# All tiles sum their attention scores in PSUM, and softmax reads them there

## The chip, the cores and the metric

The kernel runs on one core of a Trainium2 chip. Its time is the device time of one execution in microseconds (us), and several executions are compared by their median. A core has five engines with queues of their own: PE (matmuls, whose weight loads the profile shows as PEld), DVE (elementwise work and reductions), ACT (activation functions and copies), POOL, and SP, which here issues the DMAs. An engine takes its queue in order; semaphores hold an instruction until what it needs is done.

## What is computed

Attention over keys and values that are averaged in groups of 8, then two feed-forward layers over all 4608 tokens. All is float32.

```python
# attention: q, k, v of shape (8 batches, 8 heads, 576, 64)
k_p = k.reshape(B, H, Sp, 8, D).mean(axis=3)        # Sp = 72
v_p = v.reshape(B, H, Sp, 8, D).mean(axis=3)
scores = (1 / sqrt(D)) * q @ k_p.T                   # (8, 8, 576, 72)
scores = scores - max(scores, axis=-1)
attn = exp(scores); attn = attn / (sum(attn, -1) + 1e-9)
x = attn @ v_p                                       # as (4608, 512)
# first layer, 512 -> 768 -> 512
h = max(x @ w1, x @ w2, x @ w3); x = h @ w_out
# second layer, 512 -> 2048 -> 512
h = x @ w_in; x = (h - tanh(h)) @ w_out2
```

To keep float32 accuracy with the faster `float32r` matmuls, each operand is split in a high part H and a rest L, and a product is the sum of three matmuls: H·H, H·L and L·H.

## The kernel before

**Tiles.** The 576 tokens of a batch are cut into five tiles, four of 128 tokens and one of 64, in two units that meet where a block of 512 tokens of the next layer ends; 40 tiles in all, numbered from 0. A tile n is computed in two halves g = 0 and 1 of four heads each: `qk(n, g)` makes the scores of two pairs of heads (a pair p has 2 x 72 = 144 score columns), `sm_exp(n, g)` the maximum of each head (DVE, L304) and four exponentials with their sums (ACT, L307), `sm_div(n)` divides (DVE, L315 to L317) and copies the columns past 128 (ACT, L319), `tr(n)` transposes on PE (L335, L346) and splits the result (ACT L337 and L348, DVE L338 and L349). When a unit is through, `av` multiplies with the values (PE L356 to L359) and splits the output into the next layer's input (ACT L363, DVE L364).

**Two forms of `qk`.** The queries are the stationary operand: `qH` (128 rows, as many columns as the tile has tokens) is loaded into PE, and the keys `kbd` stream through it as two blocks of 144 columns, high and low part beside each other.

- The first 8 tiles (`NDIR = 8`) take the direct form: per pair three matmuls of 144 columns, qH·kH, qH·kL and qL·kH (L275 to L277), add up in one place of PSUM. Both pairs of a half share one PSUM tile of the pool `ps2` (tag `sc`, two buffers), and maximum and exponential read it there.
- The other 32 tiles take the form with two halves beside each other: one matmul of 288 columns gives qH·kH and qH·kL side by side (L283), one of 144 columns adds qL·kH to the first (L285). ACT copies the second half to SBUF (L287), DVE adds it to the first and writes the score to SBUF (L288), where maximum and exponential read it. Each pair takes a PSUM tile of its own, and it is free again after the addition.

**Order.** Attention, the preparation of weights and the first matmuls of the first layer run side by side. A list of steps (`qk`, `sm_exp`, `sm_div`, `tr`, `av`, loads) is worked off in pieces between the groups of the first layer (`moe_group`: 12 matmuls of 512 columns, L523 to L525, the result taken by ACT L527 or DVE L529), as `moe_part` paces it. Between them stand the steps of `Conv`, which turn 64-bit weights into float32: one ACT and four DVE instructions each (L94, L101 to L107) and for the first 18 weights a split (ACT L128, DVE L129). The builder's scheduler then puts the instructions of each engine into a final order, which need not be the order in which they were written. After the last tile come only matmuls with 512 columns: the rest of the first layer, its output (L657 to L659) and the second layer (L715 to L730).

Of the kernel before, what the change touches and what calls it, by code (L numbers as in the profile page):

```python
# [7 lines left out]
F32 = mybir.dt.float32  # L8
# [5 lines left out]
ALU = mybir.AluOpType  # L14
# [4 lines left out]
SP = S // POOL  # L19
# [4 lines left out]
NP = NH // 2  # L24
W2 = 2 * SP
# [9 lines left out]
NC2 = FF2 // 128  # L35
LAG = 3
LEAD = 0.3
NDIR = 8
RAWS = 3

TANH_T = 0.6
# [11 lines left out]
def moe_chain_kernel(ctx, tc, qt, kt, vm, vl, ident, cst, w123, wo1, win, wout, out):  # L53
    nc = tc.nc
    V, A, G, T, Q = nc.vector, nc.scalar, nc.gpsimd, nc.tensor, nc.sync
# [3 lines left out]
    def pool(name, bufs=1, side="left", **kw):  # L59
        cm = tc.tile_pool(name=name, bufs=bufs, side=side, **kw)  # L60
        stacks[name] = cm
        return cm.__enter__()
# [6 lines left out]
    ps2 = pool("ps2", bufs=2, space=PS)  # L69
# [70 lines left out]
    at = pool("at", side="right")  # L140
# [103 lines left out]
    qraw, qsp, sct, eT = {}, {}, {}, {}  # L244
# [19 lines left out]
    scp, nbs = {}, {}  # L264

    def qk(n, g):

        cnt = tiles[n][2]
        h, l = qsp[n]
        kb = kbd[tiles[n][0] % 2]  # L270
        if n < NDIR:
            ps = scp[n, g] = ps2.tile([128, 512], F32, tag="sc", name="ps_sc")
            for p in (2 * g, 2 * g + 1):
                o = ps[:cnt, p % 2 * W2:p % 2 * W2 + W2]
                T.matmul(o, h[:, p, :cnt], kb[:, p, 0], start=True, stop=False)  # L275
                T.matmul(o, h[:, p, :cnt], kb[:, p, 1], start=False, stop=False)
                T.matmul(o, l[:, p, :cnt], kb[:, p, 0], start=False, stop=True)  # L277
            return
        if g == 0:
            sct[n] = at.tile([128, NP, W2], F32, tag="sc", name="sc", bufs=2)  # L280
        for p in (2 * g, 2 * g + 1):
            ps = ps2.tile([128, 512], F32, tag="sc", name="ps_sc")
            T.matmul(ps[:cnt, :2 * W2], h[:, p, :cnt], kb[:, p].rearrange("p a k -> p (a k)"),  # L283
                     start=True, stop=False)
            T.matmul(ps[:cnt, :W2], l[:, p, :cnt], kb[:, p, 0], start=False, stop=True)  # L285
            tmp = at.tile([128, W2], F32, tag="sct", name="sct", bufs=2)
            A.copy(tmp[:cnt], ps[:cnt, W2:2 * W2])  # L287
            V.tensor_tensor(out=sct[n][:cnt, p], in0=ps[:cnt, :W2], in1=tmp[:cnt], op=ALU.add)  # L288

    lft = {}  # L290

    def sm_exp(n, g):
        cnt = tiles[n][2]
        if g == 0:
            if n < NDIR:
                sct[n] = at.tile([128, NP, W2], F32, tag="sc", name="sc", bufs=2)
            nbs[n] = (at.tile([128, NH], F32, tag="nb", name="nb", bufs=2),
                      at.tile([128, NH], F32, tag="su", name="su", bufs=2))
        s = sct[n][:cnt].rearrange("p c (h k) -> p (c h) k", k=SP)
        nb, su = (t[:cnt] for t in nbs[n])  # L300
        src = (scp.pop((n, g))[:cnt, :2 * W2].rearrange("p (h k) -> p h k", k=SP) if n < NDIR else
               s[:, 4 * g:4 * g + 4])
        c = slice(4 * g, 4 * g + 4)
        V.tensor_reduce(out=nb[:, c], in_=src, axis=AX.X, op=ALU.max, negate=True)  # L304
        for h in range(4):
            i = 4 * g + h
            A.activation(s[:, i], src[:, h], AF.Exp, bias=nb[:, i:i + 1], scale=1.0,  # L307
                         accum_out=su[:, i:i + 1])
# [108 lines left out]
    for n in range(ntl + 1):  # L417
        last = n == ntl
        if not last:
            b = tiles[n][0]  # L420
            k = n - first_tile[b]
# [10 lines left out]
        if not last:  # L432
            add(qk, n, 0)
            add(sm_exp, n, 0)
        if n:
            add(sm_div, n - 1)
        if not last:
            add(qk, n, 1)
            if aux:
                add(*aux.pop(0))  # L440
            add(sm_exp, n, 1)
# [268 lines left out]
    def h2(j, c):  # L710
        ps = psc.tile([128, 512], F32, tag="mm", name="ps_mm", bufs=3)
        wh, wl_ = (t.rearrange("p (a b) -> p a b", b=128) for t in wt[2 * c])
        for kc in range(NE):
            xh, xl2 = ct[j * NE + kc][0]
            T.matmul(ps, wh[:, kc], xh, start=(kc == 0), stop=False)  # L715
            T.matmul(ps, wh[:, kc], xl2, start=False, stop=False)  # L716
            T.matmul(ps, wl_[:, kc], xh, start=False, stop=(kc == NE - 1))  # L717
        return ps
# [22 lines left out]
    for i in range(len(seq) + LAG):  # L741
        if i < len(seq):
            j, c = seq[i]
            ps = h2(j, c)
# [67 lines left out]
```

## Time and profile before

| | |
|---|---|
| device time, median of 3 runs | 1552.76 us (1550.59 to 1554.56) |
| span of the profiled execution, first to last instruction | 1548.8 us |
| PE busy | 1508.3 us, 97% of the span |
| weight loads of PE (beside the matmuls) | 1250.4 us, 81% |
| DVE busy | 1154.0 us, 75% |
| ACT busy | 823.5 us, 53% |
| POOL busy | 195.5 us, 13% |

The span is one execution under the profiler; what lies around it (1552.76 - 1548.8 = 4.0 us against the median) is start and end of the program. Busy times of PE are the lengths of its matmuls as modelled, and these overlap; how much of PE's time a matmul takes is the distance from its start to the next one's. In the rows, "idle before" is the time in which the engine had nothing to run, and the name behind the arrow is what ended it.

### The profile page before, as it was taken

What the parts mean: (1) busy time and instruction counts of PE and PEld (TensorE: products, weight loads), DVE (VectorE), ACT (ScalarE), POOL (GpSimd) and SP (SyncE); (2) the same over time, 40 slices, a digit from 0 to 9 for tenths busy, and PEclk for the clock granted to TensorE, in tenths of its full rate; (3) what the DMA queues carried; (4) which work ended last, traced back from release to release, by engine and by line L of the source; (5) the groups of instructions that cost most, each with busy time, mean ns of one, the idle gap of its engine ahead of it and who ended that gap; (6) DMA issues with size and microseconds to landing.
All of it is one profiled execution on the core that took longest, in us unless ns stands there. A gap on an engine that the chain in (4) does not pass through costs nothing.

```text
span 1548.8 us, 20108 instructions
## 1 busy us (share of the span) xinstructions
PE 1508.3 (97%) x6896; PEld 1250.4 (81%) x6896; DVE 1154.0 (75%) x2050; ACT 823.5 (53%) x2059; POOL 195.5 (13%) x223
## 2 busy tenths in 40 slices
PE   4899999999999999999999999999999999999999
PEld 4678878888888788888888888888888888888887
DVE  7998378777777831533488888888888888888886
ACT  7664266555566510632455555555555555555554
POOL 4503020202100110920001000010101000010000
PEclk9889999999999999999999999999999999999999
DMA  7645144545332511955300000010100000010000
GB/s 260 182 136 173 58 138 145 173 147 180 123 120 96 182 50 51 328 188 174 123 1 28 28 28 28 1 55 0 55 1 28 28 28 28 0 55 0 28 1 28
DMA packets 68614, 134.55 MB, mean 87 GB/s; under 512 B 11552, under 2 KB 11680, under 8 KB 68512
## 3 DMA queue, kind: packets, MB, share of 16 engines
q1 hardware_dynamic: 68512, 133.27, 26.5%
q8 instruction: 54, 0.88, 0.2%
q14 instruction: 48, 0.39, 0.1%
HBM read 91.82 MB, written 41.42 MB: 86 GB/s over the span
## 4 chain that ended last, share of the span: by engine, by line
PE 89%; DVE 8%; ACT 1%; issue 1%; DMA 0%; ACTq 0%; DVEq 0%; SPq 0%
PE ps_mm L715 8%; PE ps_mm L717 8%; PE ps_acc L730 8%; PE ps_acc L728 8%; PE ps_acc L729 8%; PE ps_mm L716 8%; PE ps_mm L523 8%; PE ps_mm L524 8%; PE ps_mm L525 8%; PE ps_acc L659 2%; PE ps_acc L658 2%; PE ps_acc L657 2%; PE ps_mm L659 1%; PE ps_mm L658 1%; PE ps_mm L657 1%; PE ps_sc L283 1%
## 5 line engine op out<-in xcount | busy, mean ns | idle before, releaser
L523 PE MATMUL ps_mm<-xH,wH 128*128 128x512 f32 x648 | 260.0, 402 | 0.0
L524 PE MATMUL ps_mm<-xL,wH 128*128 128x512 f32 x648 | 254.2, 392 | 0.0
L525 PE MATMUL ps_mm<-xH,wL 128*128 128x512 f32 x648 | 253.8, 392 | 0.0
L703 ACT CAST gH<-w 128x512 fp32r<-128x512 f32 x144 | 89.4, 621 | 301.3 <-DVE w L702 301.3
L715 PE MATMUL ps_mm<-ioH,ctH 128*128 128x512 f32 x576 | 224.2, 389 | 0.8 <-ACT ioH L614 0.8
L717 PE MATMUL ps_mm<-ioH,ctL 128*128 128x512 f32 x576 | 224.1, 389 | 0.0
L716 PE MATMUL ps_mm<-ioL,ctH 128*128 128x512 f32 x576 | 224.1, 389 | 0.0
L728 PE MATMUL ps_acc<-ctH,gH 128*128 128x512 f32 x576 | 224.1, 389 | 0.0
L729 PE MATMUL ps_acc<-ctL,gH 128*128 128x512 f32 x576 | 224.1, 389 | 0.0
L730 PE MATMUL ps_acc<-ctH,gL 128*128 128x512 f32 x576 | 224.1, 389 | 0.0
L704 DVE TENSOR_TENSOR gL<-w,gH 128x512 fp32r<-128x512 f32 x144 | 103.9, 722 | 92.1 <-ACT gH L703 86.5
L529 DVE TENSOR_TENSOR h<-h,ps_mm 128x512 f32<-128x512 f32 x108 | 73.9, 685 | 104.2 <-PE ps_mm L525 102.9
L525 PEld LDWEIGHTS ps_mm<-xH,wL 128*128 128x128 f32 x648 | 121.9, 188 | 25.9
L615 POOL TENSOR_TENSOR ioL<-ioL,ioH 128x512 fp32r<-128x512 f32 x32 | 49.3, 1558 | 728.9 <-ACT ioH L614 728.9
L523 PEld LDWEIGHTS ps_mm<-xH,wH 128*128 128x128 f32 x648 | 122.6, 189 | 22.7
L524 PEld LDWEIGHTS ps_mm<-xL,wH 128*128 128x128 f32 x648 | 122.4, 189 | 22.5 <-DVE xL L364 0.3
L715 PEld LDWEIGHTS ps_mm<-ioH,ctH 128*128 128x128 f32 x576 | 108.2, 188 | 23.7 <-ACT ioH L614 1.2
L729 PEld LDWEIGHTS ps_acc<-ctL,gH 128*128 128x128 f32 x576 | 108.1, 188 | 22.6
L717 PEld LDWEIGHTS ps_mm<-ioH,ctL 128*128 128x128 f32 x576 | 108.1, 188 | 22.5
L730 PEld LDWEIGHTS ps_acc<-ctH,gL 128*128 128x128 f32 x576 | 108.1, 188 | 22.4
L716 PEld LDWEIGHTS ps_mm<-ioL,ctH 128*128 128x128 f32 x576 | 108.1, 188 | 22.4
L728 PEld LDWEIGHTS ps_acc<-ctH,gH 128*128 128x128 f32 x576 | 108.0, 188 | 22.3
(106 smaller groups left out, 2843.9 us busy)
## 6 DMA issues: line engine op xcount, KB each, us to landing
hs<-h SPq DMA_DIRECT2D x54, 256.0 KB, 2.0
ioL<-hs SPq DMA_DIRECT2D x54, 256.0 KB, 3.2
kraw<-kt SPq DMA_DIRECT2D x32, 288.0 KB, 3.3
raw<-w SPq DMA_DIRECT2D x18, 512.0 KB, 3.8
xs<-ob SPq DMA_DIRECT2D x36, 256.0 KB, 2.1
ioL<-xs SPq DMA_DIRECT2D x36, 256.0 KB, 3.4
out<-ob SPq DMA_DIRECT2D x36, 256.0 KB, 2.2
qraw<-qt SPq DMA_DIRECT2D x32, 256.0 KB, 3.0
```

The costliest lines, as they stand in the source:

```text
L523: T.matmul(ps[:, :BA], wH[i][:, kc], xh[:, kc], start=(kc == 0), stop=False)
L524: T.matmul(ps[:, :BA], wH[i][:, kc], xl[:, kc], start=False, stop=False)
L525: T.matmul(ps[:, :BA], wL[i][:, kc], xh[:, kc], start=False, stop=(kc == NE - 1))
L529: V.tensor_tensor(out=t, in0=t, in1=ps[:, :BA], op=ALU.max)
L703: A.copy(gH, w)
L704: V.tensor_tensor(out=gL, in0=w, in1=gH.bitcast(F32), op=ALU.subtract)
L715: T.matmul(ps, wh[:, kc], xh, start=(kc == 0), stop=False)
L716: T.matmul(ps, wh[:, kc], xl2, start=False, stop=False)
L717: T.matmul(ps, wl_[:, kc], xh, start=False, stop=(kc == NE - 1))
L728: T.matmul(acc, gH[:, r], oh, start=(c == 0), stop=False)
L729: T.matmul(acc, gH[:, r], ol, start=False, stop=False)
L730: T.matmul(acc, gL[:, r], oh, start=False, stop=(c == NC2 - 1))
```

## The change

`NDIR` and the second form are gone: all 40 tiles take the direct form. For the 32 tiles from the ninth on, each pair of heads has three matmuls of 144 columns where it had one of 288 and one of 144, the copy L287 and the addition L288 are gone, the two pairs of a half share one PSUM tile, and maximum (L304) and exponential (L307) read PSUM where they read SBUF. The exponential still writes `sc` in SBUF. Lines of the changed kernel after L290 have numbers that are lower by 15.

```diff
-NDIR = 8
     def qk(n, g):
...
-        if n < NDIR:
-            ps = scp[n, g] = ps2.tile([128, 512], F32, tag="sc", name="ps_sc")
-            for p in (2 * g, 2 * g + 1):
-                o = ps[:cnt, p % 2 * W2:p % 2 * W2 + W2]
-                T.matmul(o, h[:, p, :cnt], kb[:, p, 0], start=True, stop=False)
-                T.matmul(o, h[:, p, :cnt], kb[:, p, 1], start=False, stop=False)
-                T.matmul(o, l[:, p, :cnt], kb[:, p, 0], start=False, stop=True)
-            return
-        if g == 0:
-            sct[n] = at.tile([128, NP, W2], F32, tag="sc", name="sc", bufs=2)
+        ps = scp[n, g] = ps2.tile([128, 512], F32, tag="sc", name="ps_sc")
         for p in (2 * g, 2 * g + 1):
-            ps = ps2.tile([128, 512], F32, tag="sc", name="ps_sc")
-            T.matmul(ps[:cnt, :2 * W2], h[:, p, :cnt], kb[:, p].rearrange("p a k -> p (a k)"),
-                     start=True, stop=False)
-            T.matmul(ps[:cnt, :W2], l[:, p, :cnt], kb[:, p, 0], start=False, stop=True)
-            tmp = at.tile([128, W2], F32, tag="sct", name="sct", bufs=2)
-            A.copy(tmp[:cnt], ps[:cnt, W2:2 * W2])
-            V.tensor_tensor(out=sct[n][:cnt, p], in0=ps[:cnt, :W2], in1=tmp[:cnt], op=ALU.add)
+            o = ps[:cnt, p % 2 * W2:p % 2 * W2 + W2]
+            T.matmul(o, h[:, p, :cnt], kb[:, p, 0], start=True, stop=False)
+            T.matmul(o, h[:, p, :cnt], kb[:, p, 1], start=False, stop=False)
+            T.matmul(o, l[:, p, :cnt], kb[:, p, 0], start=False, stop=True)
...
     def sm_exp(n, g):
...
-            if n < NDIR:
-                sct[n] = at.tile([128, NP, W2], F32, tag="sc", name="sc", bufs=2)
+            sct[n] = at.tile([128, NP, W2], F32, tag="sc", name="sc", bufs=2)
...
-        src = (scp.pop((n, g))[:cnt, :2 * W2].rearrange("p (h k) -> p h k", k=SP) if n < NDIR else
-               s[:, 4 * g:4 * g + 4])
+        src = scp.pop((n, g))[:cnt, :2 * W2].rearrange("p (h k) -> p h k", k=SP)
```

The scheduler's order changes with it, from the tile numbered 8 (the ninth, of 64 tokens) on. Three places matter below.

On PE, one half of a tile of 128 tokens between matmuls of the first layer, before (a name is output<-inputs, and the size is the output's):

```order
L525 MATMUL ps_mm<-xH,wL_157 128x512
L283 MATMUL ps_sc<-kbd_167,qH 128x288
L285 MATMUL ps_sc<-kbd_167,qL 128x144
L283 MATMUL ps_sc<-kbd_167,qH 128x288
L285 MATMUL ps_sc<-kbd_167,qL 128x144
L523 MATMUL ps_mm<-xH,wH_139 128x512
```

and in the changed kernel (L273 to L275 are the three matmuls, L508 to L510 those of the first layer):

```order
L510 MATMUL ps_mm<-xH,wL_157 128x512
L273 MATMUL ps_sc<-kbd_167,qH 128x144
L274 MATMUL ps_sc<-kbd_167,qH 128x144
L275 MATMUL ps_sc<-kbd_167,qL 128x144
L273 MATMUL ps_sc<-kbd_167,qH 128x144
L274 MATMUL ps_sc<-kbd_167,qH 128x144
L275 MATMUL ps_sc<-kbd_167,qL 128x144
L508 MATMUL ps_mm<-xH,wH_139 128x512
```

Four matmuls have become six, and they still stand in one piece.

On DVE, from the division of tile 7 on (L317; L129, L103 and L105 prepare weights, L288 adds scores, L304 takes a maximum, L338 and L349 split the transposed tile 7), before:

```order
L317 TENSOR_TENSOR sc<-sc,su 128x576
L288 TENSOR_TENSOR sc<-ps_sc,sct 64x144
L129 TENSOR_TENSOR wL_154<-ma,wH_136 128x512
L103 TENSOR_SCALAR ma<-ma 128x512 x2
L288 TENSOR_TENSOR sc<-ps_sc,sct 64x144
L188 TENSOR_REDUCE ksum<-kraw 128x72
L304 TENSOR_REDUCE nb<-sc 64x4
L338 TENSOR_TENSOR eL<-ps_tr,eH 128x4x128
L349 TENSOR_TENSOR eX<-ps_tr,eX 32x2x128
L259 TENSOR_TENSOR qL<-qraw,qH 128x512
L188 TENSOR_REDUCE ksum<-kraw 128x72
L315 TENSOR_SCALAR su<-su 64x8
```

and in the changed kernel (L302 is the division, L289 the maximum, L323 and L334 the two splits, L128 and L104 prepare weights):

```order
L302 TENSOR_TENSOR sc<-sc,su 128x576
L187 TENSOR_REDUCE ksum<-kraw 128x72
L289 TENSOR_REDUCE nb<-ps_sc 64x4
L128 TENSOR_TENSOR wL_154<-ma,wH_136 128x512
L323 TENSOR_TENSOR eL<-ps_tr,eH 128x4x128
L334 TENSOR_TENSOR eX<-ps_tr,eX 32x2x128
L258 TENSOR_TENSOR qL<-qraw,qH 128x512
L187 TENSOR_REDUCE ksum<-kraw 128x72
L300 TENSOR_SCALAR su<-su 64x8
L104 SCALAR_TENSOR_TENSOR ma<-raw,ma 128x512
```

The additions are gone, the two L103 have moved behind the next division, and one L105 (now L104) has come forward. From here to the division of tile 8 both have the update of the keys (L201, now L200), the first maximum of tile 9 and a reciprocal; before it also two additions of scores, in the changed kernel also the second maximum of tile 9.

On DVE again, before the division of tile 16 (L317; ahead of it a group of the first layer, L529, and a preparation of weights, L101 to L107, with scores and a maximum of tile 17 in between), before:

```order
L316 RECIPROCAL su<-su 128x8
L529 TENSOR_TENSOR h<-h,ps_mm 128x512
L101 TENSOR_SCALAR ma<-ma 128x512
L288 TENSOR_TENSOR sc<-ps_sc,sct 64x144
L103 TENSOR_SCALAR ma<-ma 128x512
L288 TENSOR_TENSOR sc<-ps_sc,sct 64x144
L105 SCALAR_TENSOR_TENSOR ma<-raw,ma 128x512
L304 TENSOR_REDUCE nb<-sc 64x4
L107 SCALAR_TENSOR_TENSOR ma<-raw,ma 128x512
L317 TENSOR_TENSOR sc<-sc,su 128x576
```

and in the changed kernel (division L302; L514 is the group of the first layer, L323 and L334 split the transposed tile 15, the preparation begins with L100):

```order
L300 TENSOR_SCALAR su<-su 128x8
L301 RECIPROCAL su<-su 128x8
L302 TENSOR_TENSOR sc<-sc,su 128x576
L514 TENSOR_TENSOR h<-h,ps_mm 128x512
L323 TENSOR_TENSOR eL<-ps_tr,eH 128x4x128
L334 TENSOR_TENSOR eX<-ps_tr,eX 32x2x128
L187 TENSOR_REDUCE ksum<-kraw 128x72
L514 TENSOR_TENSOR h<-h,ps_mm 128x512
L100 TENSOR_SCALAR ma<-ma 128x512
```

The division stands right behind its sums and reciprocal now, ahead of the whole preparation of weights.

## Rows read from the trace of the kernel before

**Rows 1.** The page: the whole span.

```profile
span 1548.8 us, 20108 instructions
```

**Rows 2.** Busy time (instructions) of each engine by stretch, granted clock, DMA.

```profile
68.00:86.00 18.00, 11.67 (x53) 8.16 (x52) 17.16 (x39) 14.23 (x63) 8.54 (x15) 0.72 0.58 184
86.00:515.00 429.00, 422.75 (x2109) 352.57 (x2109) 325.89 (x728) 239.80 (x904) 49.99 (x84) 1.00 0.42 134
515.00:1548.80 1033.80, 1029.14 (x4539) 851.36 (x4538) 752.67 (x1163) 521.39 (x906) 106.32 (x70) 1.00 0.17 57
```

**Rows 3.** Waits of PE's weight loads, 68 to 515 us: total, times, longest.

```profile
PEld ps_sc L283 <- DVE sc L288: 5.3, 7, 1.8
PEld ps_av L356 <- DVE xL L364: 4.8, 7, 1.9
PEld ps_tr L335 <- DVE sc L317: 4.2, 3, 1.9
```

**Rows 4.** Timeline of PE: start, length, instruction; the direct form, six matmuls.

```profile
49.67 0.23 PE L275 MATMUL ps_sc<-kbd,qH 128*128 128x144 f32 x1
...
50.07 0.27 PE L276 MATMUL ps_sc<-kbd,qH 128*128 128x144 f32 x1
50.18 0.28 PE L277 MATMUL ps_sc<-kbd,qL 128*128 128x144 f32 x1
50.29 0.44 PE L523 MATMUL ps_mm<-xH,wH 128*128 128x512 f32 x1
```

**Rows 5.** Timeline of PE: the form with two halves, four matmuls, 128 tokens.

```profile
302.29 0.29 PE L283 MATMUL ps_sc<-kbd,qH 128*128 128x288 f32 x1
...
302.73 0.44 PE L523 MATMUL ps_mm<-xH,wH 128*128 128x512 f32 x1
```

**Rows 6.** Timeline of PE: the same form, 64 tokens.

```profile
314.90 0.29 PE L283 MATMUL ps_sc<-kbd,qH 128*64 128x288 f32 x1
315.04 0.23 PE L285 MATMUL ps_sc<-kbd,qL 128*64 128x144 f32 x1
...
315.30 0.44 PE L523 MATMUL ps_mm<-xH,wH 128*128 128x512 f32 x1
```

**Rows 7.** Groups by line and shape: count | busy us, mean ns | idle before.

```profile
L307 ACT ACTIVATE sc<-sc,nb 128x72 f32<-128x72 f32 x200 | 68.7, 345 | 36.1 <-DVE nb L304 36.1
L105 DVE SCALAR_TENSOR_TENSOR ma<-raw,ma 128x512 int32<-128x512 int32 x56 | 40.0, 716 | 0.2
L283 PE MATMUL ps_sc<-kbd,qH 128*128 128x288 f32 x100 | 29.2, 338 | 2.7 <-DVE sc L288 2.6
L288 DVE TENSOR_TENSOR sc<-ps_sc,sct 128x144 f32<-128x144 f32 x100 | 28.1, 301 | 18.0 <-ACT sct L287 17.5
L304 DVE TENSOR_REDUCE nb<-sc 128x4 f32<-128x288 f32 x50 | 22.4, 448 | 0.8
L307 ACT ACTIVATE sc<-ps_sc,nb 128x72 f32<-128x72 f32 x56 | 17.2, 324 | 1.9 <-DVE nb L304 1.9
L304 DVE TENSOR_REDUCE nb<-ps_sc 128x4 f32<-128x288 f32 x14 | 6.2, 444 | 0.4 <-PE ps_sc L277 0.3
```

**Rows 8.** Timeline of PE, waits at tiles 8 to 10 [idle before <-releaser].

```profile
76.54 0.61 PE L283 MATMUL ps_sc<-kbd,qH 128*128 128x288 f32 x1 [1.53 <-DVE sc L288]
79.33 0.70 PE L285 MATMUL ps_sc<-kbd,qL 128*128 128x144 f32 x2 [2.19 <-DVE qL L259]
...
82.91 0.69 PE L335 MATMUL ps_tr<-idt,sc 64*128 64x64 f32 x4 [1.14 <-DVE sc L317]
...
84.86 0.74 PE L356 MATMUL ps_av<-eH,VH 128*128 128x448 f32 x1
```

**Rows 9.** Timeline of DVE, from the division of tile 7 to that of tile 8.

```profile
72.71 1.08 DVE L317 TENSOR_TENSOR sc<-sc,su 128x576 f32<-128x576 f32 x1
...
74.53 1.74 DVE L103 TENSOR_SCALAR ma<-ma 128x512 int32<-128x512 int32 x2
76.19 0.29 DVE L288 TENSOR_TENSOR sc<-ps_sc,sct 64x144 f32<-64x144 f32 x1
...
82.11 0.74 DVE L317 TENSOR_TENSOR sc<-sc,su 64x576 f32<-64x576 f32 x1
```

**Rows 10.** Timeline of PE, two later waits.

```profile
212.84 0.36 PE L356 MATMUL ps_av<-eH,VH 128*128 128x192 f32 x1 [1.69 <-DVE xL L364]
...
229.09 0.66 PE L335 MATMUL ps_tr<-idt,sc 128*128 128x128 f32 x4 [1.55 <-DVE sc L317]
```

## The prediction

> **What bounds the kernel now.** I read the busy time by stretch first. From 515 us on PE runs 1029.1 of 1033.8 us [rows 2], on matmuls that the change does not touch; so the end moves by as much as PE reaches that point earlier or later. Ahead of it PE is idle for 6.3 us between 86 and 515 us and for another 6.3 between 68 and 86, where the granted clock averages 0.72, that is, a part of the stretch at the lower level of 1.2 GHz [rows 2]. The first eight tiles, up to 68 us, have the same form before and after, and their instructions stand in the same order. So the question is how many microseconds of PE's time the new form costs, and how many of these 12.6 idle ones it gives back. I read the waits next: PE's weight loads wait for the additions of scores (5.3 us), the split of the attention output (4.8) and the division (4.2), all on DVE [rows 3], which is busy 17.2 of the 18 us of the early stretch [rows 2].
>
> **PE pays.** The columns are the same: 288 + 144 before, 3 x 144 after. What is new is a matmul with a weight load per pair. The timeline shows both forms at the full clock. In the direct form the six matmuls of a half take from 49.67 to 50.29 us, 0.62 us until the next matmul starts, and they start 0.11 apart, which is more than 144 columns take (0.06, from the two starts below) and so is the load of 128 weight columns [rows 4]. In the form with two halves the four take from 302.29 to 302.73, 0.44 us [rows 5]. A half costs 0.18 us more. L283 ran 100 times on tiles of 128 tokens [rows 7], two to a half, so 50 halves: 50 x 0.18 = 9.0 us. In tiles of 64 tokens the four matmuls take 0.40 us (314.90 to 315.30), and one of 144 columns 0.06 with half as many weights to load (the second starts at 315.04 as the first of 288 columns took 0.14, and the four sum up as 0.14 + 0.06 twice) [rows 6]; six of them take 6 x 0.065 = 0.39, no more than before. The changed order keeps the six in one piece between matmuls of 512 columns, as it kept the four, so nothing hides the loads there. Four of the 50 halves (tiles 9 and 10) fall between 72 and 90 us, where PE waits for others: 0.7 us hidden. PE's share is **+8.3 us**, and this term is measured, not guessed; if nothing is hidden it is 9.0.
>
> At this place the Trainium skill speaks differently. Its page "TensorE: Matmul & The Clock Gate", section "Back-to-back issue gap", gives about 81 ns per matmul for a steady stream with 128 columns; by it six would take 0.49 us and the term would be 50 x 0.05 = 2.5 us. The 0.11 us between starts in rows 4 is what this kernel's `float32r` loads take, and I go by it.
>
> **What DVE and ACT save.** 128 additions at 0.30 us (the mean of L288 [rows 7]) leave DVE and as many copies leave ACT. The maximum costs the same from either memory (444 and 448 ns), the exponential is a little shorter from PSUM (324 against 345) [rows 7]. None of this counts by itself, since both engines are idle often; it counts where PE waits.
>
> **The stretch of tiles 8 to 10.** Here PE has done its matmuls of the first layer and waits in turn for additions, for the split of a query tile and for a division (1.53, 2.19 and 1.14 us), until the product with the values starts at 84.86 [rows 8]; from there on it is busy. The path runs over DVE from the division of tile 7 to that of tile 8, 72.71 to 82.11 us [rows 9]. By the two orders, four additions of this path go (4 x 0.30), the two L103 (74.53 to 76.19, 1.66 us [rows 9]) move behind it, and one L105 (0.72) and the second maximum of tile 9 (0.45 [rows 7]) come in: -1.2 - 1.66 + 0.72 + 0.45 = -1.7 us. The clock is a second part of it. A mean of 0.72 over 18 us means about 10 us at the lower level (1 - 0.5 x 10/18), in which PE is busy for some 6.5 us (11.7 x 10/18 [rows 2]) and loses half of that, 3.2 us, at most; a shorter idle stretch could spare a part, and I take 0.5. Together **-2.2 us**. Bounds: at best the three waits of rows 8 go (-4.9 in all), at worst the new order puts PE behind half of ACT's eight exponentials of tile 9 (4 x 0.35) and loses 1.4 us.
>
> **The later waits.** Between 86 and 515 us 6.3 us are idle, and stretches between back-to-back matmuls add little. The wait of 1.55 us at 229.09 [rows 10] is for the division of tile 16, which stood behind a preparation of weights; in the changed order it stands ahead of it, with the transposes still 24 matmuls behind the scores, so this wait goes. The wait of 1.69 us at 212.84 [rows 10] is for the split of the output (L364), which still has a preparation of weights in front of it: it stays. Of the other 3 us I take half, since the loads that wait for additions (5.3 us, most of it early [rows 3]) have nothing left to wait for but exponentials done long before. That is **-3.1 us**. Bounds: -6.3, all gone, and +1, since a new order can make new waits of about the size of one of these.
>
> **What a PSUM tile now waits for.** A half's tile used to be free after the addition; now it is held until the fourth exponential: 0.45 for the maximum and 4 x 0.35 for exponentials, about 1.9 us. There are two tiles for two halves, so the next use is a full tile later. In the steady part twelve matmuls of the first layer stand between the halves (12 x 0.23 = 2.7 us, by 1029.1 us for 4539 matmuls [rows 2]), and the same engine order feeds them, so I cost this at nothing; without that cover each half would wait for up to 1.9 us.
>
> **Sum.** +8.3 - 2.2 - 3.1 = +3.0 us on the profiled span of 1548.8 us [rows 1]; what lies around the span (4.0 us against the median of 1552.76) does not change. Forecast: 1552.76 + 3.0 = **1555.8 us**, 0.2% more. A measurement of this kernel can tell about 0.3%, 4.7 us, from no change; so the likeliest verdict is no difference.
>
> **The rivals.**
>
> - *The waits only move (slower).* The new order removes DVE work that was not what PE waited for, and each wait ends with the next thing in the queue. Then the loads alone count: +8.3 us, 1561.1 us. For it: DVE stays near full in the early stretch with weights to prepare, and waits for L364 are not touched. Against it: the division at 229.09 has plainly moved. It decides if less than 3.6 us of the 12.6 idle ones come back. Chance 0.27.
> - *The banks are held too long (slower).* PE waits at the first matmul of a half for the exponential that reads the same PSUM tile, at the places where halves follow each other closely: the tiles at 72 to 90 us and pairs of halves without matmuls between them. Against it: a tile's two halves have a buffer each, so only the half after next can wait. At 1 us for some five such places the time would be 1561 + 5 = 1566 us. It decides as soon as ACT is over 2 us behind PE there. Chance 0.06.
> - *All idle time comes back (faster).* If DVE and ACT are relieved enough, the 12.6 us go and with them 2 of the 3.2 us that the lower clock can cost: 8.3 - 14.6 = -6.3, 1546.5 us. Against it: 4.8 us of the waits are for L364, whose place in the queue is as before. Chance 0.06.
> - *The loads hide as in a steady stream.* If the third load of a pair were as cheap as 0.05 us per half, the term is 2.5 and the sum 2.5 - 5.3 = -2.8, 1550.0 us, still within 0.3%. That is the result of the page's 81 ns named above. Rows 4 speak against it. Chance 0.03.
>
> **How the numbers follow.** The forecast has 0.58, and its own spread (1551 to 1557.5) lies within 0.3%. With the rival of the hidden loads, no difference has 0.61; slower by over 0.3% is 0.27 + 0.06 = 0.33; faster 0.06. The range has to reach the first rival: from 1550.5 us (PE's +9.0 with both best bounds, -4.9 and -6.3, is -2.2) to 1562 us (+9.0 and no gain at all is 1561.8). It leaves out the banks and the full gain, and some of the edges.
>
> **What the profile of the changed kernel would show.** Right: six starts 0.11 us apart in each half of 128 tokens, L276's kind of load in the list of groups with about 128 more entries; DVE about 38 us less busy; the wait at tile 16's transposes gone; the start of the product with the values near 83 us; PE's idle time between 86 and 515 us near 3 us. The last stretch, from the end of attention on, should be as long as before (1033.8 us). Wrong would be: weight loads closer than 0.11 us; new waits of PE for L307 (then L292) of over 3 us in all; or an early stretch that ends later than before at the lower clock.

## The result and the profile after

The changed kernel took 1561.82 us, median of 4 runs (1560.85 to 1562.33); the kernel before took 1551.67 in the same session (1549.23 to 1554.56). The ratio is 1.0065, 95% interval 1.0053 to 1.0077: slower by 0.65%, about 10 us. The forecast was 1555.8 with a range of 1550.5 to 1562.0. The time lies 6.0 us above the forecast and only 0.2 us inside the range, beside the number of the first rival, "the waits only move" (1561.1).

The span and the three stretches of the changed kernel, with the columns of [rows 2]. The middle stretch is cut where attention ends, 10 us later than before:

```profile
span 1558.9 us, 20133 instructions
...
68.00:86.00 18.00, 11.25 (x68) 8.81 (x66) 17.75 (x36) 13.85 (x63) 9.69 (x18) 0.88 0.65 200
86.00:525.00 439.00, 433.16 (x2230) 364.50 (x2231) 302.15 (x609) 209.90 (x783) 51.87 (x84) 0.99 0.40 131
525.00:1558.90 1033.90, 1029.23 (x4540) 851.48 (x4538) 751.28 (x1162) 522.20 (x905) 109.71 (x70) 1.00 0.17 57
```

The last stretch is 1033.9 us, as in [rows 2]: the whole loss arises ahead of it. In the middle stretch PE is busy for 10.4 us more than in [rows 2], and still idle for 5.8 us, against 6.3. Some 1.7 us of the busy time is work that came over late from the stretch before (see the product with the values below). So PE has more to do there and has got almost none of its idle time back. The waits of its weight loads, 68 to 525 us, answer to [rows 3]:

```profile
PEld ps_tr L320 <- issue: 7.7, 5, 3.6
PEld ps_av L341 <- DVE xL L349: 4.3, 7, 1.9
...
PEld ps_sc L275 <- DVE qL L258: 2.3, 2, 1.7
...
PEld ps_sc L273 <- ACT sc L292: 0.5, 1, 0.5
```

The waits for additions are gone, as they must be. The wait for the split of the output is hardly shorter (4.8 before). The wait of the transposes, which had 4.2 us for the division in [rows 3], has grown to 7.7; PE's own waits name the division for it, 6.1 us in two waits, both in the early stretch below. The wait for the split of a query tile (L258) is no new kind: before, it was

```profile
PEld ps_sc L285 <- DVE qL L259: 3.0, 2, 2.5
```

But most of it now falls at another place, tile 12. A wait for the exponentials that hold a PSUM tile, the second rival, hardly shows (0.5 us in all).

The steady part: PE's timeline through one half of 128 tokens, beside [rows 5].

```profile
308.78 0.23 PE L273 MATMUL ps_sc<-kbd,qH 128*128 128x144 f32 x1
308.85 0.28 PE L274 MATMUL ps_sc<-kbd,qH 128*128 128x144 f32 x1
308.97 0.27 PE L275 MATMUL ps_sc<-kbd,qL 128*128 128x144 f32 x1
...
309.41 0.44 PE L508 MATMUL ps_mm<-xH,wH 128*128 128x512 f32 x1
```

The six matmuls take 0.63 us (308.78 to 309.41), the four of before took 0.44. This is the term that the forecast called measured, and it is there. The early stretch, beside [rows 8] and [rows 9]: first PE, then DVE.

```profile
75.95 0.63 PE L320 MATMUL ps_tr<-idt,sc 128*128 128x128 f32 x4 [2.62 <-DVE sc L302]
79.71 0.33 PE L275 MATMUL ps_sc<-kbd,qL 128*128 128x144 f32 x1 [0.53 <-DVE qL L258]
84.31 0.66 PE L320 MATMUL ps_tr<-idt,sc 64*128 64x64 f32 x4 [3.49 <-DVE sc L302]
...
86.58 0.74 PE L341 MATMUL ps_av<-eH,VH 128*128 128x448 f32 x1
```

```profile
74.57 1.24 DVE L302 TENSOR_TENSOR sc<-sc,su 128x576 f32<-128x576 f32 x1
...
76.76 0.93 DVE L128 TENSOR_TENSOR wL<-ma,wH 128x512 fp32r<-128x512 f32 x1
...
78.77 0.88 DVE L258 TENSOR_TENSOR qL<-qraw,qH 128x512 fp32r<-128x512 f32 x1
...
80.91 1.55 DVE L200 SCALAR_TENSOR_TENSOR kbd<-ksum,kbd 64x288 fp32r<-64x288 f32 x2
...
83.43 0.74 DVE L302 TENSOR_TENSOR sc<-sc,su 64x576 f32<-64x576 f32 x1
```

Three waits of 4.9 us in [rows 8] have become three of 6.6 us; with two waits of 0.57 and 0.55 us in this stretch that [rows 8] does not show, it was 6.0. The path over DVE from one division to the next takes 8.86 us (74.57 to 83.43) where it took 9.40 (72.71 to 82.11 [rows 9]). It is 0.5 us shorter, not 1.7: four of its instructions take longer than the same ones before, whose rows there are, besides 1.08 for the division [rows 9],

```profile
73.94 0.67 DVE L129 TENSOR_TENSOR wL<-ma,wH 128x512 fp32r<-128x512 f32 x1
...
78.58 0.69 DVE L259 TENSOR_TENSOR qL<-qraw,qH 128x512 fp32r<-128x512 f32 x1
...
80.77 0.94 DVE L201 SCALAR_TENSOR_TENSOR kbd<-ksum,kbd 64x288 fp32r<-64x288 f32 x2
```

that is 0.16 + 0.26 + 0.19 + 0.61 = 1.2 us. The product with the values starts at 86.58 instead of 84.86 all the same, because the path began 1.86 us later (74.57 against 72.71), behind instructions that are the same in both kernels; the last experiment takes this up. Further on, two places:

```profile
136.80 0.34 PE L275 MATMUL ps_sc<-kbd,qL 128*128 128x144 f32 x1 [1.51 <-DVE qL L258]
...
234.17 0.61 PE L320 MATMUL ps_tr<-idt,sc 128*128 128x128 f32 x4
```

The transposes of tile 16, which waited 1.55 us in [rows 10], come without a wait, as forecast. But PE now stops between the second and the third matmul of tile 12, where before it was idle for 0.1 us. The experiments lead back to that place.

### The profile page after: what moved, and what is told of

It reads as the page before. It is cut to its first block, busy times and chain, and to the rows that moved or that the text cites. A ratio compares the mean times of both kernels' runs of the same rounds, so it can differ in the third digit from the quotient of the medians.

```text
span 1558.9 us, 20133 instructions
## 1 busy us (share of the span) xinstructions
PE 1518.0 (97%) x7024; PEld 1263.2 (81%) x7024; DVE 1127.3 (72%) x1922; ACT 792.9 (51%) x1931; POOL 201.3 (13%) x223
## 4 chain that ended last, share of the span: by engine, by line
PE 89%; DVE 6%; DMA 1%; ACT 1%; POOL 1%; issue 1%; SPq 0%; POOLq 0%; ACTq 0%; DVEq 0%
PE ps_mm L700 8%; PE ps_acc L715 8%; PE ps_mm L701 8%; PE ps_mm L702 8%; PE ps_acc L714 8%; PE ps_acc L713 8%; PE ps_mm L508 8%; PE ps_mm L510 8%; PE ps_mm L509 8%; PE ps_acc L644 2%; PE ps_acc L642 2%; PE ps_acc L643 2%; PE ps_mm L644 1%; PE ps_mm L642 1%; PE ps_mm L643 1%; DMA vraw<-vm 1%
## 5 line engine op out<-in xcount | busy, mean ns | idle before, releaser
L508 PE MATMUL ps_mm<-xH,wH 128*128 128x512 f32 x648 | 261.0, 403 | 0.0
L510 PE MATMUL ps_mm<-xH,wL 128*128 128x512 f32 x648 | 254.6, 393 | 0.0
L514 DVE TENSOR_TENSOR h<-h,ps_mm 128x512 f32<-128x512 f32 x108 | 73.9, 685 | 123.6 <-PE ps_mm L510 119.2
L510 PEld LDWEIGHTS ps_mm<-xH,wL 128*128 128x128 f32 x648 | 122.4, 189 | 26.7
L508 PEld LDWEIGHTS ps_mm<-xH,wH 128*128 128x128 f32 x648 | 123.2, 190 | 22.2
L292 ACT ACTIVATE sc<-ps_sc,nb 128x72 f32<-128x72 f32 (+1 forms) x320 | 98.4, 322 | 72.2 <-DVE nb L289 72.0
```

The source lines that it names most:

```text
L508: T.matmul(ps[:, :BA], wH[i][:, kc], xh[:, kc], start=(kc == 0), stop=False)
L510: T.matmul(ps[:, :BA], wL[i][:, kc], xh[:, kc], start=False, stop=(kc == NE - 1))
```

## The experiments

Twelve kernels were run. In each session the kernel before ran beside them on the same chip; its medians were 1551.0, 1552.5 and 1551.3 us. All ratios are to it.

**The two halves of the change, one at a time.** `pe_only` pays without relief: the kernel before, with the matmul of 288 columns split in two; copies and additions stay.

```
-            T.matmul(ps[:cnt, :2 * W2], h[:, p, :cnt], kb[:, p].rearrange("p a k -> p (a k)"),
-                     start=True, stop=False)
+            T.matmul(ps[:cnt, W2:2 * W2], h[:, p, :cnt], kb[:, p, 1], start=True, stop=True)
+            T.matmul(ps[:cnt, :W2], h[:, p, :cnt], kb[:, p, 0], start=True, stop=False)
```

> The kernel before, with PE's part of the change alone: on the tiles from the ninth on, the matmul of 288 columns is two matmuls of 144 (the low keys first, into the second half of the PSUM tile), so a half has six weight loads where it had four; ACT's copies and DVE's additions stay. Theory A (the loads are the loss, and the relief of DVE and ACT brings almost nothing): 50 halves of 128 tokens x 0.18 us, less some hidden, so 8 to 9.5 us slower than before, six starts 0.11 us apart in each half. Theory B (a good part of the loss is new waits on the PSUM tiles that the changed kernel holds until the exponentials are done): 4 to 6 us slower, the rest of the 10 us is absent here. Theory C (the relief gives some 3 us back in the changed kernel, as predicted, and something else takes it away again): 11 to 13 us slower, since the loads stand here without any relief.

`relief_only` has relief without pay: the changed kernel without the product of the high queries and the low keys in any tile.

```
-            T.matmul(o, h[:, p, :cnt], kb[:, p, 1], start=False, stop=False)
```

> The changed kernel without the matmul of the high queries with the low keys (qH by kL is left out of the score), so that a half has four weight loads again, as before the change, while copies and additions are gone and maximum and exponential read PSUM. PE's four matmuls of 144 columns take about 0.4 us (0.06 + 3 x 0.11) where the four before took 0.44: up to 2 us less over 50 halves. Theory A (loads alone): 1 to 3 us faster than before, so 11 to 13 us faster than the changed kernel. Theory B (new waits on PSUM tiles): 2 to 4 us slower than before. Theory C (the relief does give 3 us): 4 to 6 us faster than before.

Measured: `pe_only` 1578.69 us, ratio 1.0181 (1.0167 to 1.0195), 27.7 us slower, beyond every expectation. `relief_only` 1551.08 us, ratio 0.9998 (0.9989 to 1.0007): with 128 additions and copies fewer and no load more, nothing is gained. The two do not add up to the change. `pe_only` shows one large stop in PE's timeline, at the same tile 12 as the changed kernel; the row of ACT is the preparation of the first layer's last weights, from the same kernel:

```profile
140.24 0.33 PE L285 MATMUL ps_sc<-kbd,qL 128*128 128x144 f32 x1 [3.96 <-DVE qL L259]
```

```profile
132.25 0.66 ACT L94 ACTIVATE ma<-raw 128x512 f32<-128x512 f32 x1 [5.86 <-DMA raw<-w]
```

**Is the price of a load right?** Two kernels put extra small matmuls into the second layer, where PE never waits and nothing of the scores is near: low weights by low inputs, 96 groups, added to a running sum (their product is negligible beside it). `extra_four` has the shape of the form before, `extra_six` that of the form after.

```
+            if kc < 2 and (j * NC2 + c) % 3 == 0:
+                for a in (0, 2):
+                    y, z = ct[j * NE + a][0][1], ct[j * NE + a + 1][0][1]
+                    T.matmul(ps[:, :288], wl_[:, a], y[:, :288], start=False, stop=False)
+                    T.matmul(ps[:, :144], wl_[:, a + 1], z[:, :144], start=False, stop=False)
```

and, for `extra_six`, against `extra_four`:

```
-                    T.matmul(ps[:, :288], wl_[:, a], y[:, :288], start=False, stop=False)
+                    T.matmul(ps[:, :144], wl_[:, a], y[:, :144], start=False, stop=False)
+                    T.matmul(ps[:, 144:288], wl_[:, a], y[:, 144:288], start=False, stop=False)
```

> The kernel before with, at 48 places of the second layer, two extra groups of four small matmuls (288, 144, 288 and 144 columns, low weights by low inputs, added to a running sum); it stands beside extra_six and is its base. TensorE is busy without a gap there, and no step of the scores is touched. The group of four took 0.44 us in the steady part of the kernel before: 96 groups should bring 42 us, 1593 us, under every theory.

> As extra_four, with each matmul of 288 columns split into two of 144 with the same weights: the same columns, two weight loads more in each of 96 groups. Theory A (a load behind a matmul of 144 columns costs time by itself, 0.18 us for the two in a group): 17 us over extra_four. Theory B (loads hide as in a steady stream and the cost in the scores came from their waits): 0 to 4 us over extra_four. Theory C (the jump of 28 us of pe_only is the price of the loads, 0.55 us for two): 50 us over.

Measured: 1601.08 us, ratio 1.0319 (1.0303 to 1.0335), and 1617.27, 1.0417 (1.0403 to 1.0431). The difference is 16.2 us for 96 groups, 0.17 us each. PE's timeline has a group of `extra_four` first, then one of `extra_six`, each with the matmul behind it:

```profile
1013.81 0.30 PE L721 MATMUL ps_mm<-ioL,ctL 128*128 128x288 f32 x1
...
1014.25 0.44 PE L715 MATMUL ps_mm<-ioH,ctH 128*128 128x512 f32 x1
```

```profile
1003.29 0.23 PE L721 MATMUL ps_mm<-ioL,ctL 128*128 128x144 f32 x1
...
1003.92 0.44 PE L715 MATMUL ps_mm<-ioH,ctH 128*128 128x512 f32 x1
```

0.44 us for four, 0.63 for six, at a place without any wait. Theory A holds: two loads cost 0.18 us, 50 halves cost 8.9. So the 27.7 us of `pe_only` are not the price of its loads.

**Which tiles lose?** `ndir11` has the new form for tiles 8 to 10 alone, `late_only` for tile 11 and all after it, `hybrid64` for the later tiles of 64 tokens, where the six matmuls cost no more than the four.

```
-NDIR = 8
+NDIR = 11                                         # ndir11
...
-        if n < NDIR:
+        if direct(n):                             # late_only and hybrid64
...
+        return n < NDIR or n > 10                 # direct(n) in late_only
+        return n < NDIR or tiles[n][2] == 64      # direct(n) in hybrid64
```

> The changed form for tiles 8, 9 and 10 alone, where weight preparation is thickest; the later tiles keep the split form. As predicted, the early stretch should gain 2.2 and pay about 0.4 of loads: 1549.2 against 1551. If the early gain is only what the traces show, half a microsecond: 1550.5 to 1551.5, no difference that can be told. If the new waits are set off by these three tiles: 1553 to 1555.

> The changed form for tile 11 and all later ones; tiles 8 to 10 keep the split form of before. As predicted: loads 8.1, less 3.1 of later waits, 1556. If the waits only move: loads alone and a new wait at 131 to 136 us, 1559 to 1562, nearly all of the loss of the changed kernel. If the order of the instructions decides by accident, as the 28 us of pe_only hint: anything up to 1575.

> The kernel before, with the direct form in the first 8 tiles and, new, in the 7 later tiles of 64 tokens, where six loads of 64 columns take no longer than four matmuls did (0.40 us); the 25 later tiles of 128 tokens keep the two halves. Theory A (loads of 128 columns are the whole loss): within 1.5 us of before. Theory B (holding PSUM tiles until the exponentials costs): 1 to 3 us slower. Theory C (relief helps): 1 to 2 us faster.

Measured: `ndir11` 1560.40 us, ratio 1.0048 (1.0036 to 1.0061); `late_only` 1559.82, 1.0056 (1.0041 to 1.0070); `hybrid64` 1557.82, 1.0041 (1.0027 to 1.0054). Each part loses nearly what the whole loses. For three tiles whose loads cost 0.7 us (four halves of 128 tokens) `ndir11` loses 7.9 us, and `hybrid64` loses 6.8 for no load at all. Their traces show a stop at one and the same place. In `ndir11`, from its cause to PE (SPq is SP's queue of DMA issues; the row's length is how long the issue took):

```profile
124.27 2.39 SPq L211 DMA_DIRECT2D vraw<-vm  x2
126.76 0.37 SPq L88 DMA_DIRECT2D raw<-w  x1
```

```profile
131.27 0.66 ACT L94 ACTIVATE ma<-raw 128x512 f32<-128x512 f32 x1 [5.12 <-DMA raw<-w]
```

```profile
131.96 0.43 DVE L101 TENSOR_SCALAR ma<-ma 128x512 f32<-128x512 f32 x1 [4.13 <-ACT ma L94]
...
138.22 1.29 DVE L259 TENSOR_TENSOR qL<-qraw,qH 128x512 fp32r<-128x512 f32 x2
```

```profile
138.96 0.34 PE L285 MATMUL ps_sc<-kbd,qL 128*128 128x144 f32 x1 [4.05 <-DVE qL L259]
```

Read from the top: the load of the last first-layer weights (`raw<-w`) stands on SP's queue behind two value loads (`vraw<-vm`), which wait for buffers that POOL's sums free: after 120.2 us the queue issues nothing until 124.27 (the trace names L207 on POOL for 2.4 us of that wait). The weights are issued at 126.76 us and have landed by 131.27, when ACT, which has stood still for 5.12 us, goes on. Behind ACT stand exponentials and the high part of the next tile's transposes; DVE waits 4.13 us for ACT; the query split comes at 138.22, and PE stops for 4.05 us. The trace names DVE as what PE waits for, but the wait goes back over DVE and ACT to a load on SP's queue. The same load in the kernel before stands between the two value loads:

```profile
123.76 0.35 SPq L211 DMA_DIRECT2D vraw<-vm  x1
124.22 0.37 SPq L88 DMA_DIRECT2D raw<-w  x1
```

```profile
128.04 0.68 ACT L94 ACTIVATE ma<-raw 128x512 f32<-128x512 f32 x1 [0.81 <-DMA raw<-w]
```

There ACT waits 0.81 us and PE 0.1. But the place on SP's queue is not all of the difference. PE of `ndir11` is 1.9 us behind already at the transposes of tile 10, and counted from there the load goes out only 0.6 us later than before and lands 1.4 us later. What differs more is DVE's order: in `ndir11` it takes these weights (L101 at 131.96) ahead of the query split (L259 at 138.22), in the kernel before behind it:

```profile
131.75 0.93 DVE L259 TENSOR_TENSOR qL<-qraw,qH 128x512 fp32r<-128x512 f32 x1
...
135.67 0.62 DVE L101 TENSOR_SCALAR ma<-ma 128x512 f32<-128x512 f32 x1
```

So a late load costs PE time where the new order puts the work on it ahead of what PE needs. In `hybrid64` the load goes out at 128.96, behind a value load that comes only at 128.51:

```profile
128.96 0.37 SPq L88 DMA_DIRECT2D raw<-w  x1
```

```profile
132.99 0.66 ACT L94 ACTIVATE ma<-raw 128x512 f32<-128x512 f32 x1 [5.70 <-DMA raw<-w]
```

```profile
136.04 0.49 PE L288 MATMUL ps_sc<-kbd,qL 128*128 128x144 f32 x1 [4.23 <-DVE qL L259]
```

Here DVE has these weights behind the query split, as before; the load itself is late, and on ACT it holds up the transposes' high part, for which DVE waits 3.8 us. None of these edits touches a DMA. The scheduler orders the whole program anew for each of them, on SP, ACT and DVE.

**Does that queue cause the loss?** The same edit on four kernels: the first two value loads of batch 3 are held until the last weight load of the first layer has been issued, and are kept behind it on SP's queue: the loads trade places.

```
+    held = [True, []]
...                                # where the weights are loaded
+                if (self.n, i) == (18, 17):
+                    held[0] = False
+                    while held[1]:
+                        held[1].pop()()
...
     def v_load(b, p):
...
+        if b == 3 and p < 2:
+            tc.keep_in_program_order(r)
...                                # where the next value load is chosen
+            if b == 3 and i < 2 and held[0]:
+                held[1].insert(0, lambda: v_load(b, i))
+            elif i < NP:
```

The edit moves more than these loads. In the kernel before, PE, DVE and ACT keep their order with it, instruction by instruction. In the other three PE does too, but for four matmuls of `hybrid64`, while about 80 of DVE's 1900 to 2000 instructions and 27 to 51 of ACT's stand elsewhere between 76 and 144 us.

> ndir11 with one edit: the two value loads that stand ahead of the last weight load of the first layer on SP's queue are issued behind it, so that the weights no longer wait for buffers that POOL frees. Theory Q (the loss of ndir11 is that queue: the weight load issued at 126.76, ScalarE waiting 5.1 us for it, VectorE 4.1 behind it, TensorE 4.2 for the query split): the wait at 134.6 to 139.0 and the low clock after it, 5.7 us, go, and 1560.4 becomes 1554 to 1556. Theory R (the order of the instructions is an accident of the early tiles, wherever the weights stand): the wait comes elsewhere, 1559 to 1562.

> hybrid64 with the same edit. Its wait at 131.5 to 136.0 is 4.4 us, followed by 2.8 us at low clock, and there too ScalarE waits 5.7 us for the weights. Theory Q: 7 us less than its 1557.8, 1551. Theory R: 1556 to 1560.

> The changed kernel with the same edit. There the last weight load stands ahead of these value loads already (issued at 121.81), and ScalarE waits 0.4 us for it; the 1.5 us for the query split at 135 come from VectorE's own queue of weight preparation. Theory Q: 1558 to 1562, no gain over the changed kernel's 1559.6 to 1561.8. If the place of the value loads matters in another way: 1554 to 1557.

> The kernel before with the same edit, the base of the three others: its weight load is issued at 124.22 between two value loads, ScalarE waits 0.8 us, TensorE 0.3 for the query split. Theory Q: nothing to gain there, 1550 to 1552. If it is faster by over 4 us the edit does something else than take that wait away.

Measured:

| edit on | without it | with it | ratio with it, 95% interval |
|---|---|---|---|
| `ndir11` | 1560.40 | 1552.00 | 0.9999 (0.9989 to 1.0008) |
| `hybrid64` | 1557.82 | 1551.53 | 0.9999 (0.9990 to 1.0008) |
| changed kernel | 1561.82, 1559.59 | 1557.50 | 1.0037 (1.0023 to 1.0050) |
| kernel before | 1551.3 | 1551.16 | 0.9995 (0.9986 to 1.0004) |

The times without it are of the earlier sessions. Theory Q's times came: `ndir11` and `hybrid64` lose their whole loss, 8.4 and 6.3 us, and the kernel before is as fast as it was. In the trace of `ndir11_hold` the load goes out 10 us earlier, and the two waits behind it shrink (the edit moves line numbers by 5 to 7):

```profile
116.81 0.33 SPq L89 DMA_DIRECT2D raw<-w  x1
```

```profile
120.24 0.68 ACT L99 ACTIVATE ma<-raw 128x512 f32<-128x512 f32 x1 [0.87 <-DMA raw<-w]
```

```profile
133.81 0.33 PE L292 MATMUL ps_sc<-kbd,qL 128*128 128x144 f32 x1 [0.58 <-DVE qL L266]
```

By the starts of the transposes, `ndir11_hold` gains 5.5 us on `ndir11` at this stop. That the stop is the wait for the weights is shown by the chain in the trace and by the edit together; the edit alone could not tell it from a luckier order on DVE and ACT.

The changed kernel gained too, 2 to 4 us, where Theory Q had said nothing would be gained: the expectation that its weight load "stands ahead already" looked only at ACT's wait of 0.4 us. Its load is not late: it goes out at 121.81 us, earlier than the 124.22 of the kernel before. But here too DVE takes these weights (L100) ahead of the query split (L258). First the changed kernel, then the query split with the edit and PE's matmul behind it:

```profile
126.94 0.41 DVE L100 TENSOR_SCALAR ma<-ma 128x512 f32<-128x512 f32 x1
...
135.75 1.80 DVE L258 TENSOR_TENSOR qL<-qraw,qH 128x512 fp32r<-128x512 f32 x2
```

```profile
133.43 1.29 DVE L265 TENSOR_TENSOR qL<-qraw,qH 128x512 fp32r<-128x512 f32 x2
```

```profile
134.18 0.34 PE L282 MATMUL ps_sc<-kbd,qL 128*128 128x144 f32 x1
```

With the edit the load goes out at 117.62 us and DVE begins on these weights at 124.00; the query split comes earlier, and PE's wait at tile 12 is gone (the last row). By the starts of the transposes, the edit gains at two places and nowhere else after 125 us: 1.5 to 1.7 us at tile 12, and 1.6 us between tiles 14 and 15. At the second place PE waits as long with the edit as without (1.7 and 0.5 us), but in the two profiles without it the granted clock falls for a while (mean 0.83 over 210 to 220 us in `after_again`), and with it the clock stays at 1.00. Whether that fall belongs to the order or to the execution, no run tells.

`late_only` has a relative of the stop, one weight load earlier: ACT waits 6.14 us for weights at 125.57, PE 2.4 us at tile 12. Its cause is not a late issue: that load goes out at 118.95, as before (119.00), but lands 6.5 us later, where the same load took 4.2 before. `late_only` was not tried with the edit, nor was `pe_only`.

**The same kernel again.** `after_again` is the changed kernel unchanged.

> The changed kernel once more, unchanged, for a second profile of it. In its first profile TensorE ran at the lower clock from 55 to 68 us, where the instructions are still the same as before the change, and PE was 2.3 us late there; the kernel before was at the lower clock for two shorter pieces of that stretch. If that belongs to the program, this profile shows the same piece and the 2.3 us; if it differs from execution to execution, the pieces lie elsewhere, and the profiles' spans scatter by about 2 us while the median stays 9 to 11 us above before.

Measured: 1559.59 us, ratio 1.0059 (1.0045 to 1.0072), which agrees with the first measurement. Its trace differs from the first where the two programs, and the kernel before, are still one and the same. The stretch of 45 to 68 us, in the first profile, then in the second, then in the kernel before:

```profile
45.00:68.00 23.00, 20.79 (x92) 17.77 (x91) 20.01 (x45) 15.65 (x58) 6.29 (x10) 0.71 0.44 135
```

```profile
45.00:68.00 23.00, 19.45 (x106) 16.18 (x105) 21.80 (x50) 16.85 (x69) 7.05 (x12) 0.93 0.51 151
```

```profile
45.00:68.00 23.00, 20.47 (x102) 17.02 (x102) 21.98 (x49) 16.81 (x68) 7.33 (x12) 0.85 0.56 158
```

The granted clock is 0.71, 0.93 and 0.85, and 92, 106 and 102 matmuls of PE fall in it: the first profile of the changed kernel entered the early stretch about 2 us late by this alone. The path over DVE is the same in both profiles, 8.86 and 8.84 us, the four long instructions included. A single pair of profiles cannot tell an early gain of 2 us at PE; medians can.

Why the four grew can be read from the traces. While DVE works on them, POOL sums values; the first row is from the changed kernel, beside the pair of L200 (80.91, 1.55 us). In `after_hold` POOL is idle from 74.2 us on, and the same pair takes 0.93 us (the second row), the weight and the query split 0.67 and 0.69:

```profile
80.54 1.04 POOL L204 TENSOR_TENSOR vraw<-vraw 128x256 f32<-128x256 f32 x1 [1.42 <-DMA vraw<-vm]
```

```profile
79.71 0.93 DVE L205 SCALAR_TENSOR_TENSOR kbd<-ksum,kbd 64x288 fp32r<-64x288 f32 x2
```

In the traces of all kernels together the division of a tile of 128 tokens took 0.74 to 0.76 us in each of 340 cases with POOL idle, and up to 1.55 in the 94 where POOL worked for at least 30% of it. The three others, too, grew beside POOL alone, up to about twice their length. The reductions and the instructions that read PSUM (L187, L289, L323) never did. How POOL slows them, these runs do not show.

## Why the prediction came out as it did

The sum was +8.3 (loads) - 2.2 (early stretch) - 3.1 (later waits) = +3.0; measured were +8.6 to +10.1 us in two sessions.

- **The loads: right.** 50 halves at 0.18 us. The pair of extra kernels gives 0.178 us by the starts in the trace (0.445 to 0.623 us, the mean of 96 groups each) and 0.17 by the times. By the Trainium skill (page "TensorE: Matmul & The Clock Gate", section "Back-to-back issue gap"), which gives about 81 ns per matmul in a steady stream at 128 columns, six would take an estimated 0.49 us. The run shows 0.62 us with 144 columns, and the measurement decides: the rival of the hidden loads falls.
- **The 0.7 us hidden in tiles 9 and 10:** no run here tells it apart.
- **The later waits: nearly the right size.** Between the transposes of tile 10 (125 us) and the end of the program `after_hold` falls behind `before_hold` by 5.1 us, while its 44 halves of loads in that stretch cost 44 x 0.178 = 7.8: 2.7 us come back, where 3.1 were forecast from 86 us on. Tile 16's wait went as named.
- **The early stretch: wrong.** The -2.2 us did not come. By medians `ndir11_hold`, which has this part of the change alone, stands 0.8 us behind `before_hold`, its loads included; a gain of 2.2 against at most 0.7 of loads would have put it 1.5 ahead, which the two intervals together (about 2 us) just exclude. The step that failed is the sum over DVE's path, "-1.2 - 1.66 + 0.72 + 0.45 = -1.7 us". What leaves and what enters was named rightly, but every other instruction was left at its length of before, and four of them grew by 1.2 us, the pair of L200 by 0.61 alone. That leaves 0.5 us, in the second profile of the changed kernel as in the first. All four ran while POOL summed values, which the sum did not look at; such instructions were long only then (the last experiment). The 0.5 for the clock can't be read from one pair of profiles.
- **What the sum did not have.** The stop at tile 12, 1.5 us in the changed kernel. The prediction followed DVE's order at tiles 8 and 16 and took its bound for the rest, "+1, since a new order can make new waits of about the size of one of these"; it did not follow the last first-layer weights over SP, ACT and DVE, whose order the change moved in front of a query split. The bound was too small: such a stop cost `ndir11` 4.05 us and a stretch at the lower clock behind it (mean 0.76 over 139 to 146 us, so 0.24 x 7 = 1.7 us).

With the edit of the queue in both kernels the change costs 1557.50 - 1551.16 = 6.3 us: 8.9 of loads less 2.6 that come back, where 8.3 - 5.3 were forecast. The medians alone give this to about 2.5 us; the 2.7 us from the traces agree. The rest of the loss, 2 to 4 us, goes with the edit: 1.5 us is the stop at tile 12, about as much the lower clock between tiles 14 and 15, whose cause is open. That the time fell inside the range was luck: the range reached up to the first rival, and the time came to its edge by a stop that the sum did not have. The first rival gave nearly the measured number, but its mechanism, loads alone with no gain elsewhere, is only half of it: some 2 to 3 us did come back, and losses that it did not name took them away again.

What stays open: `pe_only`. Its loads (8.9) and its stop at tile 12 (4, and about 1.7 at the lower clock after it, with a granted clock of 0.83 over 140 to 150 us) explain some 14 to 15 of its 28 us; the rest is spread over many small waits, and no run separates them. And `relief_only` gains nothing although its six matmuls are four (0.41 us per half); that its own wait at tile 12 (3.0 us) eats the gain is likely, but was not tried.

No kernel here is faster than the kernel before: `before_hold` and `hybrid64_hold` cannot be told from it.

## What to carry to other kernels

When a scheduler orders the program, a small edit is two edits: the one that was written, and a new order on every queue, the DMA issues among them. To size the first, measure it where nothing waits (here the extra groups, 0.178 us each) and not by undoing half of the change, which sets off a new order of its own (here 28 us). To find the second, follow a wait back past the engine that the trace names to the first queue that stands still, and compare there, too, in which order the queues on the way take their work. Then move that one instruction, in the kernel before as well, and read from the traces what else moved with it.

## What was not expected of the hardware

A value load on SP's queue that waited for a buffer held up every issue behind it: in `ndir11` the queue issued nothing from 120.2 to 124.27 us, and ACT then stood for 5.12 us, DVE for 4.13 and PE for 4.05. The division, the splits of weights and queries and the update of the keys on DVE took up to about twice their time while POOL worked (the division 1.55 us for 0.76), and never more than usual while it was idle. And the granted clock of the same instructions in the same order differed between executions, 0.71 to 0.93 over 23 us, which moves the start of what follows by 2 us.
